# Moving one chunk's attention work between the first MLP blocks, with more blocks on three chunks and a second weight slice in halves

## The chip, the cores and the metric

One core of one Trainium2 chip. The metric is device time in microseconds (us) of one execution. The profile's span, first to last instruction, is 1.7 to 1.8 us shorter than the device time of the same execution.

## The reference

Lightning attention with decay (8 heads, 4 sequences of 768, head size 64), then an MLP with exact GELU over the 3072 tokens:

```python
for b in range(nb):                                # blocks of 64 in the reference, chunks of 128 in the kernel
    intra = (q_b @ k_b.T * Dmask) @ v_b
    inter = (q_b * lam_pow) @ kv_state
    out[b] = intra + inter
    kv_state = lam_block * kv_state + (k_b * rev_pow).T @ v_b
# ...
x = out as [3072, 512]
return gelu(x @ w_in) @ w_out                      # w_in 512x2048, w_out 2048x512
```

## The kernel before

A chunk is 128 tokens of one sequence. Group 0 is the first chunk of each of the four sequences (chunks 0 to 3), group 1 the second (4 to 7), and so on to group 5. Each group's 512 tokens go through 16 MLP blocks (`mm1`, one per 128 columns of w_in, each followed by GELU on ScalarE) and then the second matmul (`mm2`). Attention of the next group is put between blocks by `visits`: a visit at `(g, i)` runs in front of block `i` of group `g`. The program order of each engine is the order of the text. The first four blocks of groups 0 and 1 run on three chunks (384 columns); the fourth chunk's 128 columns follow in one block of their own, the catch-up.

In groups 0 and 1 a chunk takes TensorE transposes of k and q, a copy of kT (ScalarE), a scaling of qT (VectorE), scores, masked scores (VectorE), outputs, and a copy of the outputs into `x_t` (ScalarE). From group 2 on the transposes are made by DMA and the copy by VectorE. The state products (`kv`) multiply the decayed k (`decay_k`) with v and update `kv_state`. The dummy matmuls of `keep_warm` only keep TensorE busy; with fewer of them (experiments 2, 7 and 8) the granted clock was still 1.00 over the first 32 us.

```python
    for item in "q0 k1 q1 k2 q2 v1 v2 k3 q3".split():
        load(int(item[1]), item[0])
# ...
    load_w_in(0, 2)
    load_w_in(2, 4)
    load(3, "v")
    for s in range(4, NK2, 4):
        load_w_in(s, s + 4)
# ...
        split = g < 2
        def mm1(kf, lo=0, n_kf=1):
            hi = T - C if split and kf < NK2 // NS and lo == 0 else T   # first 4 blocks: three chunks
# ...
        if split:
            blocks.insert(NK2 // NS, mm1(0, T - C, NK2 // NS))          # the catch-up with the fourth chunk
# ... the opening, after chunks 0 and 1:
    outputs(live[1])
    keep_warm(2)                 # dummy matmuls
    transposes(live[3])
    outputs(live[2])
    keep_warm(1)
    scores(live[3])
    keep_warm(4)
    for n in range(M):
        decay_k(live[n], nc.vector)
    make_lam_blk()
# ...
    def first_requests():                       # visit (0, 30)
        for n in (2 * M, 2 * M + 1):
            request(n)                          # GpSimd scales q, DMA transposes k and q
        for n in range(M, 2 * M):
            decay_k(live[n], nc.gpsimd)
```

## Time and profile before

| | kernel before |
|---|---|
| device time, first three runs | 214.65 us (214.28 to 214.77) |
| span of the profiled execution | 213.1 us |
| TensorE busy | 96% |
| MLP's first block starts | 18.34 us |
| block 4 starts (20.08, then blocks 2 and 3, 8 x 0.1625, and the catch-up, 16 x 0.056) | 22.28 us |
| block 8 starts (24.88, then state products, 0.44, and block 7, 0.86) | 26.18 us |

The order of instructions on TensorE, with the idle time and its releaser in brackets, tells what waited; the time from issue to landing of a load tells what could have waited. A load is asked for alone by a window around its issue, and its landing is the issue time plus the "to landing" figure. The prediction below shows those lines.

### The profile page before, as it was taken

Reading aid. Unit: us, or ns where it says so; the run is one execution under the profiler, and the core shown is the slowest. Engines: PE = TensorE matmul, PEld = TensorE weight load, DVE = VectorE, ACT = ScalarE, POOL = GpSimd, SP = SyncE. Lnnn points to the kernel's source line nnn. Section 1 sums busy time; section 2 is a strip of 40 time slices with the busy share of each in tenths; the row PEclk is TensorE's granted clock in tenths of the full one; section 3 lists DMA queues with packets and bytes.
Section 4 is the critical chain, followed back from the end, with each engine's and each line's share of the span. In section 5 each row is a group of like instructions: output and inputs, shape, how many; then the busy total and the mean of one; then the engine's idle time right before and its main releaser. Section 6 shows DMA issues by size and latency. Waiting matters only on the chain.

```text
span 213.1 us, 3522 instructions
## 1 busy us (share of the span) xinstructions
PE 204.4 (96%) x1429; PEld 104.8 (49%) x1455; DVE 76.9 (36%) x122; ACT 87.3 (41%) x152; POOL 103.3 (48%) x118
## 2 busy tenths in 40 slices
PE   7969999999999999999999999999999999999993
PEld 2535554465655445445445445445445445444452
DVE  4758320165293747138317137217132312000000
ACT  5564663343656111464321464321465221576121
POOL 7995333892997965939678795830000000000000
PEclk9999999999999999999999999999999999999999
DMA  7999999999999699999989999991330012100112
GB/s 85 141 150 196 206 206 186 154 211 142 178 87 119 72 108 115 205 167 101 136 128 157 172 131 142 130 117 67 108 74 0 3 65 82 49 3 0 49 51 97
DMA packets 100799, 24.48 MB, mean 115 GB/s; under 512 B 92976, under 2 KB 97840, under 8 KB 100784
## 3 DMA queue, kind: packets, MB, share of 16 engines
q0 software_dynamic: 78592, 13.51, 87.1%
q1 hardware_dynamic: 22192, 10.76, 24.8%
q8 instruction: 11, 0.18, 0.4%
q14 instruction: 4, 0.03, 0.1%
HBM read 27.27 MB, written 6.29 MB: 157 GB/s over the span
## 4 chain that ended last, share of the span: by engine, by line
PE 89%; POOL 4%; DMA 3%; issue 1%; DVE 1%; ACT 0%; POOLq 0%
PE h_ps L263 39%; PE o_ps L275 37%; DMA q_t<-in_q_dram 3%; PE o_ps L230 3%; PE sc_ps L197 3%; PE o_ps L224 2%; PE kv_ps L209 2%; POOL k_t L66 2%; PE o_ps L290 2%; POOL q_t L66 1%; PE t_ps L176 1%; POOL v_t L66 1%; DVE qT L182 1%; PE idle_ps L325 0%; ACT o_sb L294 0%
## 5 line engine op out<-in xcount | busy, mean ns | idle before, releaser
L263 PE MATMUL h_ps<-x_t,w_in_t 128*128 128x512 bf16 (+2 forms) x404 | 85.7, 362 | 0.6
L275 PE MATMUL o_ps<-w_out_t,g_t 128*128 128x512 bf16 x356 | 81.7, 379 | 1.0 <-issue 0.6
L265 ACT ACTIVATE g_t<-h_ps 128x512 bf16<-128x512 f32 (+1 forms) x98 | 57.7, 588 | 37.2 <-PE h_ps L263 37.0
L263 PEld LDWEIGHTS <-w_in_t 128*128 128x128 bf16 x416 | 38.5, 98 | 41.7
L275 PEld LDWEIGHTS <-g_t 128*128 128x128 bf16 x368 | 34.7, 98 | 41.1
L201 DVE TENSOR_TENSOR sc_m<-sc_ps,dmask 128x512 bf16<-128x512 f32 x48 | 30.1, 683 | 35.0 <-PE sc_ps L197 35.0
L280 ACT COPY o_sb<-o_ps 128x512 f32<-128x512 f32 x23 | 13.5, 585 | 69.9 <-PE o_ps L275 66.4
L189 POOL TENSOR_TENSOR q_hat<-q_t,lam_p 128x512 bf16<-128x512 bf16 x16 | 16.8, 1052 | 24.1 <-DMA q_t<-in_q_dram 13.6
L66 POOL DMA_DIRECT2D k_t<-in_k_dram x24 | 22.1, 919 | 5.4 <-DMA w_out_t<-in_moe_w_out_dram 1.6
L66 POOL DMA_DIRECT2D q_t<-in_q_dram x24 | 21.6, 901 | 4.4 <-DMA w_out_t<-in_moe_w_out_dram 3.3
L66 POOL DMA_DIRECT2D v_t<-in_v_dram x23 | 20.9, 911 | 3.5 <-DMA w_out_t<-in_moe_w_out_dram 1.7
L216 DVE TENSOR_TENSOR tmp<-kv_ps,state 128x512 f32<-128x512 f32 x16 | 11.0, 686 | 31.2 <-PE kv_ps L209 31.2
L169 POOL TENSOR_TENSOR k_dec<-k_t,lam_m 128x512 bf16<-128x512 bf16 x16 | 17.2, 1104 | 0.0
L236 DVE CAST x_t<-o_ps 128x512 bf16<-128x512 f32 x16 | 10.3, 682 | 10.2 <-PE o_ps L230 10.2
L217 DVE TENSOR_TENSOR state<-tmp,lam_blk 128x512 bf16<-128x512 f32 x16 | 12.6, 790 | 0.6
L325 PE MATMUL idle_ps<-idle 128*128 128x512 bf16 x29 | 10.7, 478 | 1.2 <-DVE idle L105 1.2
L182 DVE TENSOR_TENSOR qT<-t_ps,lam_q 128x512 bf16<-128x512 bf16 x8 | 5.5, 691 | 15.4 <-PE t_ps L176 15.0
L197 PEld LDWEIGHTS <-kT 64*128 64x128 bf16 x192 | 5.7, 94 | 6.5 <-issue 3.8
L197 PE MATMUL sc_ps<-qT,kT 64*128 64x128 bf16 x192 | 8.2, 218 | 0.6 <-DVE qT L182 0.2
L230 PE MATMUL o_ps<-sc_m,v_t 128*64 128x128 bf16 x192 | 8.6, 223 | 0.1
L181 ACT COPY kT<-t_ps 128x512 bf16<-128x512 bf16 x8 | 4.7, 584 | 7.4 <-PE t_ps L176 7.4
L230 PEld LDWEIGHTS <-v_t 128*64 128x64 bf16 x192 | 5.9, 109 | 2.7 <-issue 0.6
(41 smaller groups left out, 73.4 us busy)
## 6 DMA issues: line engine op xcount, KB each, us to landing
out_dram<-o_sb SPq DMA_DIRECT2D x23, 256.0 KB, 2.2
k_t<-in_k_dram POOLq DMA_DIRECT2D x24, 128.0 KB, 5.1
q_t<-in_q_dram POOLq DMA_DIRECT2D x24, 128.0 KB, 6.0
v_t<-in_v_dram POOLq DMA_DIRECT2D x23, 128.0 KB, 6.0
w_out_t<-in_moe_w_out_dram POOLq DMA_DIRECT2D x4, 512.0 KB, 16.6
w_in_t<-in_moe_w_in_dram POOLq DMA_DIRECT2D x3, 512.0 KB, 11.0
w_in_t<-in_moe_w_in_dram POOLq DMA_DIRECT2D x2, 256.0 KB, 7.1
v_f<-in_v_dram SPq DMA_DIRECT2D x1, 256.0 KB, 3.6
```

Of the source, the lines that this page charges most:

```text
L66: nc.gpsimd.dma_start(raw[n, name], chunk_of(name, n))
L169: eng.tensor_mul(c.k_dec, c.k, lam_m[:, :, None].to_broadcast((128, H, D)))
L189: nc.gpsimd.tensor_mul(q_hat, c.q, lam_p[:, :, None].to_broadcast((128, H, D)))
L197: nc.tensor.matmul(sc_ps[hi][:, hp, :], c.kT[p, hp, :], c.qT[p, hp, :], start=True, stop=True)
L201: nc.vector.tensor_mul(c.sc_m[:, :, hi, :], sc_ps[hi], dmask_r[:, :, hi, :])
L216: nc.vector.tensor_add(tmp, kv_ps, states[c.b])
L217: nc.vector.tensor_mul(new, tmp, lam_blk)
L230: nc.tensor.matmul(c.o_ps[hi * D:(hi + 1) * D, hp, :], c.v[:, 2 * hp + hi, :], c.sc_m[:, hp, hi, :], start=(c.so == 0 and hp == 0), stop=T ...
L263: nc.tensor.matmul(h_ps[:, f, :], w, x_t[:, ki, lo:hi], start=(ki == 0 and f == 0), stop=(ki == NK1 - 1), skip_group_check=True)
L265: nc.scalar.activation(g_t[:, kf:kf + n_kf, lo:hi], h_ps, ACT.Gelu)
L275: nc.tensor.matmul(om[io], g_t[:, kf, io * C:(io + 1) * C], w_out_t[:, kf, :], start=(kf == 0), stop=(kf == NK2 - 1))
L280: nc.scalar.copy(o_sb, om[io])
```

## The change

Its intent is to open the MLP earlier. Chunk 3's transposes and scores, which the first blocks don't need, move between the blocks. So that this doesn't put the catch-up with chunk 3 too early, eight blocks of group 0 rather than four run on three chunks, with two catch-ups. The weights of blocks 4 to 7 come in two loads, as the earlier opening wants blocks 4 and 5 sooner. The dummies become one group of nine. The diff in full:

```diff
--- before.py
+++ after.py
@@ -96,8 +96,8 @@
     load_w_in(0, 2)
     load_w_in(2, 4)
     load(3, "v")
-    for s in range(4, NK2, 4):
-        load_w_in(s, s + 4)
+    for lo, hi in [(4, 6), (6, 8), (8, 12), (12, 16)]:
+        load_w_in(lo, hi)
     for s in range(NS):
         load_w_out(s)
 
@@ -248,13 +248,13 @@
     def mlp_blocks(g):
         T = M * C
 
-        split = g < 2
+        split = {0: 8, 1: 4}.get(g, 0)
         x_t = xT[g]
         g_t = g_pool.tile([128, NK2, T], BF16, tag="g", name="g_t")
 
         def mm1(kf, lo=0, n_kf=1):
 
-            hi = T - C if split and kf < NK2 // NS and lo == 0 else T
+            hi = T - C if kf < split and lo == 0 else T
             def run():
                 h_ps = bank([128, n_kf, hi - lo], F32, "m", "h_ps")
                 for f in range(n_kf):
@@ -297,8 +297,8 @@
 
         parts = NK2 // 4
         blocks = [mm1(kf) for kf in range(NK2)]
-        if split:
-            blocks.insert(NK2 // NS, mm1(0, T - C, NK2 // NS))
+        for i, kf in enumerate(range(0, split, 4)):
+            blocks.insert(split - 1 + 2 * i if split > 4 else split, mm1(kf, T - C, 4))
         if g == 0:
 
             blocks += [(mm2(io, part), 4 * 512) for pair in range(0, M, 2) for part in range(parts)
@@ -348,14 +348,8 @@
     keep_warm(2)
     outputs(live[1])
     keep_warm(2)
-    transposes(live[3])
     outputs(live[2])
-    keep_warm(1)
-    scores(live[3])
-    keep_warm(4)
-    for n in range(M):
-        decay_k(live[n], nc.vector)
-    make_lam_blk()
+    keep_warm(9)
 
 
     for n in range(M, 2 * M + 2):
@@ -380,6 +374,11 @@
         for n in ns:
             next_state(live[n])
             take_state(live[n])
+
+    def late_decays():
+        for n in range(M):
+            decay_k(live[n], nc.vector)
+        make_lam_blk()
 
     def first_requests():
         for n in (2 * M, 2 * M + 1):
@@ -392,17 +391,19 @@
 
 
     visits = {
-        (0, 2): [lambda: outputs(live[3])],
-        (0, 8): [lambda: kv(0, 1)],
-        (0, 11): [lambda: kv(2, 3)],
-        (0, 25): [lambda: transposes(live[4])],
-        (0, 26): [lambda: scores(live[4])],
-        (0, 27): [lambda: transposes(live[5]), lambda: outputs(live[4])],
-        (0, 28): [lambda: scores(live[5])],
-        (0, 29): [lambda: transposes(live[6]), lambda: outputs(live[5])],
-        (0, 30): [lambda: scores(live[6]), lambda: first_requests()],
-        (0, 31): [lambda: transposes(live[7]), lambda: outputs(live[6])],
-        (0, 32): [lambda: scores(live[7])],
+        (0, 2): [lambda: transposes(live[3])],
+        (0, 3): [lambda: scores(live[3]), late_decays],
+        (0, 6): [lambda: outputs(live[3])],
+        (0, 10): [lambda: kv(0, 1)],
+        (0, 13): [lambda: kv(2, 3)],
+        (0, 26): [lambda: transposes(live[4])],
+        (0, 27): [lambda: scores(live[4])],
+        (0, 28): [lambda: transposes(live[5]), lambda: outputs(live[4])],
+        (0, 29): [lambda: scores(live[5])],
+        (0, 30): [lambda: transposes(live[6]), lambda: outputs(live[5])],
+        (0, 31): [lambda: scores(live[6]), lambda: first_requests()],
+        (0, 32): [lambda: transposes(live[7]), lambda: outputs(live[6])],
+        (0, 33): [lambda: scores(live[7])],
         (1, 1): [lambda: outputs(live[7])],
         (1, 5): [lambda: kv(4, 5)],
         (1, 7): [lambda: kv(6, 7)],
```

## The prediction

> **What bounds the kernel now.** I read the page first (busy shares, slices, chain), then the chain of waits from 0 to 60 us, then the order of instructions from 13 to 26.6 us, then the time from issue to landing of single loads. Of the page:
>
> ```profile
> PE 204.4 (96%) x1429; PEld 104.8 (49%) x1455; DVE 76.9 (36%) x122; ACT 87.3 (41%) x152; POOL 103.3 (48%) x118
> PE   7969999999999999999999999999999999999993
> PEclk9999999999999999999999999999999999999999
> PE 89%; POOL 4%; DMA 3%; issue 1%; DVE 1%; ACT 0%; POOLq 0%
> ```
>
> TensorE is 96% busy at full clock and makes 89% of the chain that ends last. Only the first three slices (16 us) have room. After 18.3 us TensorE waits for nothing worth naming, so a gain must be made before that and survive until the steady stream of weights and tokens. The chain there (start, duration, what):
>
> ```profile
> 9.63 6.28 DMA q_t<-in_q_dram
> 15.96 0.41 PE t_ps L176 x4
> 16.39 0.70 DVE qT L182
> 17.14 0.40 PE sc_ps L197 x8
> 17.91 0.59 PE idle_ps L325 x2
> 18.51 1.30 PE h_ps L263 x8
> ```
>
> The MLP opens only when chunk 3 is through: its q lands (15.9), is transposed, scaled by VectorE, scored, and four dummy matmuls follow. But the first MLP blocks use chunks 0 to 2 alone. The order of instructions shows it (start, duration, engine, line, operation, count, idle before):
>
> ```profile
> 13.66 0.60 PE L325 MATMUL idle_ps<-idle 128*128 128x512 bf16 x2
> 14.11 0.39 PE L176 MATMUL t_ps<-ident,k_t 128*128 128x128 bf16 x4
> 15.96 0.40 PE L176 MATMUL t_ps<-ident,q_t 128*128 128x128 bf16 x4 [1.47 <-DMA q_t<-in_q_dram]
> 16.29 0.41 PE L230 MATMUL o_ps<-sc_m,v_t 128*64 128x128 bf16 x8
> 16.74 0.58 ACT L234 CAST x_t<-o_ps 128x512 bf16<-128x512 f32 x1 [1.63 <-PE o_ps L230]
> 18.34 1.46 PE L263 MATMUL h_ps<-x_t,w_in_t 128*128 128x384 bf16 x8
> 19.74 0.41 PE L230 MATMUL o_ps<-sc_m,v_t 128*64 128x128 bf16 x8
> 20.23 0.58 ACT L234 CAST x_t<-o_ps 128x512 bf16<-128x512 f32 x1
> 24.88 0.61 PE L209 MATMUL kv_ps<-v_t,k_dec 128*128 128x128 bf16 x8
> ```
>
> Chunk 2's outputs (16.29) stand in program order behind the wait for chunk 3's q, though VectorE finished chunk 2's masked scores at 12.61 + 1.88 = 14.49. What else could hold the MLP is its weights. The first w_in slice, asked for by itself, shows:
>
> ```profile
> L90 POOL DMA_DIRECT2D w_in_t<-in_moe_w_in_dram x1: 834/834/834, 10.5 to 10.5; - x1
> DMA to landing us min/median/max: 6.8/6.8/6.8
> ```
>
> Issued at 10.49, landed at 17.29. That is only 1.05 us before the MLP's present start. The same view gives the others: slice blocks 2-3 at about 18.5, v of chunk 3 at 19.7, blocks 4-7 at 12.84 + 9.2 = 22.0, blocks 8-11 at 24.6, 12-15 at 27.0. So 256 KB of w_in take about 1.2 us of a queue that is backlogged throughout (206 GB/s).
>
> **What the Trainium skill says.** "TensorE: Matmul & The Clock Gate", section "Wait — 56ns, not 53.3ns?": warm back-to-back matmuls start every N/2.4 + 2.5 ns. The trace agrees: eight of 384 columns take 1.30 us (162 each), twelve of 512 take 2.59 us (216), and eight of 128 take 0.45 us (56). The same page, "HAM oscillation — how this bites in real kernels": the clock falls after idle gaps of some 3.4 us. Here the gap of 1.47 us left the granted clock at 1.00, and the change makes none so long. "ScalarE: Activation LUTs", "What ACT_TABLE_LOAD costs": an activation costs a fixed part plus 0.833 ns a column, and neighbours overlap by some 93 ns. Here 384 columns take 0.49 us, 512 take 0.60, and successive starts overlap by 0.10. "DMA: Bandwidth & Descriptors", "Anatomy of one DMA — SWDGE (gpsimd) path", gives about 2 us fixed per transfer. In this backlog landings come 1.2 us apart, so that fixed part overlaps, and halving a load should not cost it again; no run shows that yet.
>
> **The change part by part.** Let S be the start of the MLP; the place to compare is the start of block 8 with both versions having done the state products of chunks 0 and 1. In the kernel before that is 24.88 + 0.44 (state products) + 0.86 (block 7) = 26.19.
>
> Removed in front of S: chunk 3's transposes (8 x 56 ns = 0.45), the 1.47 us wait, the wait for qT, scores (0.33), and five dummies, against nine dummies in one group. Chunk 2's outputs can now start at 14.49 + 0.05 = 14.55 and take 0.34; nine dummies take 9 x 0.216 = 1.94, to 16.83. ScalarE's copy of chunk 2 ends near 15.6. The first weights land at 17.29, so S is about 17.33, set by the weights and not by the dummies. Gain at S: 18.34 - 17.33 = 1.01.
>
> Added after S: transposes 0.45 and scores 0.33 = 0.78, merely moved. The second catch-up: four blocks become 16 x 162 ns + 16 x 56 ns instead of 16 x 216 ns, that is 2.60 + 0.90 - 3.45 = 0.05. Work after S up to block 8: eight blocks 8 x 0.65 = 5.20, transposes 0.45, scores 0.33, outputs 0.34, two catch-ups 1.80, state products 0.45: 8.57, against 7.75 before (18.34 to 26.19 is 7.85, with 0.10 of waiting for v).
>
> New waits after S, by program order:
> Transposes run S+1.30 to S+1.75, block 2 to S+2.40. The q transposes of chunk 3 started at 15.96 before and their scores at 17.14, 1.18 later; now they start at S+1.52, so scores can start at S+2.70. Wait 0.30. (ScalarE copies kT after the activation of block 1, ending near S+2.5, earlier than that.)
> Scores to S+3.03, block 3 to S+3.68 = 21.0. Blocks 4-5 now need a half slice: 19.7 + 1.2 = 20.9. Wait about 0. With the whole slice at 22.0 it would have been 1.0, which is what the halving is for. Blocks 6-7 land near 22.1, wanted at 22.6.
> Outputs of chunk 3 at S+4.98; their x comes 0.45 later plus a copy of 0.58, but ScalarE is in the activation of block 5 from S+5.18 for 0.49. With the overlap of 0.10 the copy runs S+5.57 to S+6.15. TensorE has finished block 6 at S+5.97, so the first catch-up starts near S+6.22. Wait 0.25.
> Sum: 8.57 + 0.30 + 0.25 = 9.12; block 8 at 17.33 + 9.12 = 26.45, that is 0.26 later than 26.19. The decays of k move behind chunk 3's scores on VectorE; from S+4.4 they take 2.49 + 0.58 to S+7.5 = 24.8, and the state products want them near S+8.2. Off the path. Block 8's weights (24.6) are there. From here both kernels have the same work, so the end moves by the same amount.
>
> **The rivals.**
> A, the waits are smaller than I count: if TensorE loses nothing after S, block 8 starts at 25.90 and the kernel gains 0.29, to 214.35. For it: VectorE is idle before qT and the wait of 0.30 is a difference of small numbers. Against it: the 1.18 us from transposes to scores is measured on this very chunk.
> B, the whole 1.8 us between the early outputs and the old start is won (dummies end at 16.83, S there, and little is given back): 213 or so. Against it: the weights at 17.29. The queue ahead of them is unchanged, so they cannot come sooner.
> C, the extra load delays others. GpSimd runs at most eight loads open: the second w_out waits for q, the third for the first w_in, always eight back. One more load shifts w_out's first issue by a microsecond, yet all of these then sit in a backlog and land when the bytes ahead are through. Group 1's q of chunk 4 lands at 22.32 + 16.8 = 39.1 and is used at 40.45, 1.3 us of slack. If half loads move bytes more slowly by a fifth, blocks 4-5 wait some 0.3 and the time is 215.2.
> D, ScalarE becomes the bound among the first blocks: six activations of 0.49 with two copies of 0.58 need 4.1 of the first 6 us. Against it: a third is free.
>
> **Range and chances.** The sum says +0.26; A pulls down by up to 0.55, C up by 0.3, and the three runs before span 0.49. I predict 214.85 us, with 214.2 to 215.5 to hold it eight times in ten. Two per cent is 4.3 us; even a complete removal of everything idle before 18.34 is below that. Faster by over 2%: 0.01; within 2%: 0.98; slower: 0.01.
>
> **What would show it.** In the changed trace: outputs of chunk 2 near 14.55; a short idle stretch before the first MLP block ended by the w_in load, block at 17.3; 0.3 us idle before chunk 3's scores, released by VectorE's qT; about none before block 4; 0.25 idle before the first catch-up, released by ScalarE's copy of x; the state products of chunks 0 and 1 near 26.0 and block 8 near 26.45; the rest of the kernel equal, only shifted. I am wrong if S is well under 17.3 (the weights came sooner), if the second half slice makes TensorE wait, or if loads of chunks 4 and 5 run late near 40 us.

## The result, and the profile after

| | before | after |
|---|---|---|
| device time, median of four runs | 214.47 us (214.25 to 214.77) | 214.88 us (214.53 to 215.05) |
| span of the profiled execution | 213.1 us | 213.3 us |
| first w_in slice landed | 17.3 us | 16.3 us |
| MLP's first block starts | 18.34 us | 16.88 us |
| block 4 starts | 22.28 us | 20.91 us |
| block 8 starts | 26.18 us | 26.32 us |

The ratio of after to before is 1.0016, 95% interval 0.9997 to 1.0036: the same.

The page of the changed kernel: busy times first, then the chain's shares. TensorE still sets the time, but the chain now has 4% of DMA for w_in.

```profile
PE 205.5 (96%) x1450; PEld 105.9 (50%) x1475; DVE 77.7 (36%) x122; ACT 87.4 (41%) x153; POOL 104.0 (49%) x119
...
PE 88%; POOL 5%; DMA 4%; issue 1%; ACT 0%; POOLq 0%
```

The order of instructions in the opening (start, duration, engine, line, operation, count, idle before):

```profile
14.27 0.73 PE L230 MATMUL o_ps<-sc_m,v_t 128*64 128x128 bf16 x8
...
14.93 1.90 PE L325 MATMUL idle_ps<-idle 128*128 128x512 bf16 x8
...
16.88 1.46 PE L263 MATMUL h_ps<-x_t,w_in_t 128*128 128x384 bf16 x8
...
18.63 0.81 PE L263 MATMUL h_ps<-x_t,w_in_t 128*128 128x384 bf16 x4
...
18.83 0.69 DVE L182 TENSOR_TENSOR qT<-t_ps,lam_q 128x512 bf16<-128x512 bf16 x1 [4.27 <-PE t_ps L176]
...
19.57 0.40 PE L197 MATMUL sc_ps<-qT,kT 64*128 64x128 bf16 x8
...
20.91 1.47 PE L263 MATMUL h_ps<-x_t,w_in_t 128*128 128x384 bf16 x8 [0.18 <-DMA w_in_t<-in_moe_w_in_dram]
...
22.31 0.41 PE L230 MATMUL o_ps<-sc_m,v_t 128*64 128x128 bf16 x8
...
22.66 3.38 PE L263 MATMUL h_ps<-x_t,w_in_t 128*128 128x384 bf16 x40
...
25.87 0.61 PE L209 MATMUL kv_ps<-v_t,k_dec 128*128 128x128 bf16 x8
```

The MLP opens 1.46 us sooner, at the end of the dummies. (The view counts eight of the nine; some records of matmuls are missing in a trace.) From 16.88 to 26.32 are 9.44 us, of which 8.57 are work (the prediction's sum). The scores wait: block 2 is through at 18.63 + 0.65 = 19.28 and they start at 19.57, 0.29 lost. Block 3 is through at 19.91 + 0.65 = 20.56 and block 4 starts at 20.91, 0.35 lost. (The bracket says 0.18 because the ends of matmuls are modelled with their latency; starts and known spacing are the safer count.) Blocks 4 and 5 take 1.30, so the outputs at 22.31 come 0.10 late. The forty matmuls from 22.66 to 25.87 are 3.10 us of work in 3.21. That gives 0.29 + 0.35 + 0.10 + 0.11 = 0.85, and 8.57 + 0.85 = 9.42.

The chain of waits (start, duration, what) says the same in three lines. It runs back from block 4 to the issue of the load at 12.86. Nothing that TensorE did before 20.9 is on it:

```profile
12.86 8.01 DMA w_in_t<-in_moe_w_in_dram
20.86 0.05 issue
20.91 1.47 PE h_ps L263 x8
```

After block 8 both executions are alike. The last group of matmuls starts at 206.12 before and at 206.25 after, 0.13 later, as block 8 did (0.14).

### The profile page after: what moved, and what is told of

Read it like the earlier page. It is cut to its first block, busy times and chain, and to the rows that moved or that the text cites. A ratio compares the mean times of both kernels' runs of the same rounds, so it can differ in the third digit from the quotient of the medians.

```text
span 213.3 us, 3565 instructions
## 1 busy us (share of the span) xinstructions
PE 205.5 (96%) x1450; PEld 105.9 (50%) x1475; DVE 77.7 (36%) x122; ACT 87.4 (41%) x153; POOL 104.0 (49%) x119
## 4 chain that ended last, share of the span: by engine, by line
PE 88%; POOL 5%; DMA 4%; issue 1%; ACT 0%; POOLq 0%
PE h_ps L263 38%; PE o_ps L275 37%; DMA w_in_t<-in_moe_w_in_dram 4%; PE o_ps L230 3%; PE sc_ps L197 3%; PE kv_ps L209 2%; PE o_ps L224 2%; POOL k_t L66 2%; PE o_ps L290 2%; POOL q_t L66 2%; POOL v_t L66 1%; PE t_ps L176 1%; POOL w_in_t L90 1%; ACT o_sb L294 0%; POOL row L78 0%
## 5 line engine op out<-in xcount | busy, mean ns | idle before, releaser
L263 PEld LDWEIGHTS <-w_in_t 128*128 128x128 bf16 x432 | 39.2, 98 | 41.5 <-DMA w_in_t<-in_moe_w_in_dram 0.6
L66 POOL DMA_DIRECT2D k_t<-in_k_dram x24 | 22.1, 919 | 5.5 <-DMA w_in_t<-in_moe_w_in_dram 2.9
L66 POOL DMA_DIRECT2D q_t<-in_q_dram x24 | 21.6, 900 | 3.9 <-DMA w_out_t<-in_moe_w_out_dram 3.4
L169 POOL TENSOR_TENSOR k_dec<-k_t,lam_m 128x512 bf16<-128x512 bf16 x16 | 17.3, 1107 | 0.0
L217 DVE TENSOR_TENSOR state<-tmp,lam_blk 128x512 bf16<-128x512 f32 x16 | 13.5, 841 | 0.6
## 6 DMA issues: line engine op xcount, KB each, us to landing
w_out_t<-in_moe_w_out_dram POOLq DMA_DIRECT2D x4, 512.0 KB, 16.4
```

The source lines that it names most:

```text
L66: nc.gpsimd.dma_start(raw[n, name], chunk_of(name, n))
L169: eng.tensor_mul(c.k_dec, c.k, lam_m[:, :, None].to_broadcast((128, H, D)))
L217: nc.vector.tensor_mul(new, tmp, lam_blk)
L263: nc.tensor.matmul(h_ps[:, f, :], w, x_t[:, ki, lo:hi], start=(ki == 0 and f == 0), stop=(ki == NK1 - 1), skip_group_check=True)
```

## The experiments

Twelve experiments ran, five rounds each, in four calls; three of them repeat a kernel (before, after, combined). All gave correct results. Times are set against the kernel before in the same rounds; its medians were 214.76, 214.68, 214.19 and 214.86 us, with single runs from 213.91 to 216.22. Times therefore resolve about 0.3%. What is smaller is read from the traces.

This table is from one profiled execution of each. "Landed" is the load that brings block 4's weights. Block 8 starts with the state products of chunks 0 and 1 done; where these stand ahead of block 7, its start is worked out as in the table of before. "Rest" is the span minus block 8's start.

| kernel | first slice landed | MLP starts | block 4's weights landed | block 4 starts | block 8 starts | span | rest |
|---|---|---|---|---|---|---|---|
| before | 17.3 | 18.34 | 22.0 | 22.28 | 26.18 | 213.1 | 186.9 |
| after | 16.3 | 16.88 | 20.9 | 20.91 | 26.32 | 213.3 | 187.0 |
| scores later | 16.1 | 16.92 | 20.7 | 20.72 | 26.13 | 213.1 | 187.0 |
| six dummies | 16.4 | 16.49 | 20.7 | 20.68 | 26.09 | 213.2 | 187.1 |
| whole slice | 17.1 | 17.20 | 21.9 | 21.92 | 27.33 | 214.3 | 187.0 |
| v later | 15.6 | 17.01 | 19.5 | 20.68 | 26.09 | 213.0 | 186.9 |
| before, again | 16.3 | 17.32 | 22.1 | 22.16 | 26.06 | 213.0 | 186.9 |
| after, again | 17.2 | 17.24 | 21.7 | 21.79 | 27.20 | 214.1 | 186.9 |
| combined | 16.3 | 16.34 | 19.0 | 19.82 | 25.23 | 212.9 | 187.7 |
| before, no dummies | 17.0 | 17.17 | 21.6 | 21.74 | 25.64 | 212.6 | 187.0 |
| scores of 8, 9 later | 17.0 | 17.00 | 19.6 | 20.49 | 25.90 | 212.8 | 186.9 |
| decays on VectorE | 16.8 | 16.84 | 19.4 | 20.32 | 25.73 | 212.9 | 187.2 |
| combined, again | 16.3 | 16.36 | 19.1 | 19.84 | 25.25 | 212.8 | 187.6 |
| decays first | 16.6 | 16.67 | 20.2 | 20.28 | 25.87 | 214.5 | 188.6 |

Theory 1 was that the arrival of block 4's weights fixes block 4, so that a head start runs into it. Theory 2 was that every wait and every microsecond of head start counts by itself.

### 1. Scores one block later

```diff
-        (0, 3): [lambda: scores(live[3]), late_decays],
+        (0, 4): [lambda: scores(live[3]), late_decays],
```

> The changed kernel with chunk 3's scores one block later (after block 3 instead of after block 2). Theory 1 (the arrival of w_in blocks 4-5 near 20.9 us fixes block 4): the 0.29 us in which TensorE waits for kT/qT before the scores goes, the wait before block 4 grows by the same, block 4 still starts when its weights land, 20.9 +- 0.2, and the time is that of the changed kernel within 0.1 us (about 214.9). Theory 2 (each wait is a loss of its own): about 0.3 us faster than the changed kernel, about 214.6.

Measured: 214.68 us, ratio to the kernel before 0.9997 (0.9972 to 1.0023). The wait for qT before the scores is gone (0.09 us is left between block 3 and the scores). TensorE then waits for the weights, the time from the end of the scores, 20.06 + 0.33 = 20.39, to 20.72, when they land at 20.7. Block 8 is 0.19 us earlier than after, and all of it is that in this execution the load landed 0.2 sooner. Theory 1 holds in the trace; the times alone couldn't have told a gain of 0.3 us.

### 2. Six dummies

```diff
-    keep_warm(9)
+    keep_warm(6)
```

> The changed kernel with six instead of nine dummy matmuls before the MLP. In the changed kernel's trace the MLP opened at 16.88 because the dummies ended there; its first weights had landed at 16.3. Theory 1 (arrival of blocks 4-5 fixes block 4): the MLP opens up to 0.5 us earlier, the wait before block 4 grows by as much, time unchanged within 0.1 us (214.9). Theory 2 (the start of the MLP carries through): 0.4 to 0.6 us faster, about 214.4.

Measured: 214.84 us, 1.0007 (0.9978 to 1.0035). In order of instructions:

```profile
16.49 1.47 PE L263 MATMUL h_ps<-x_t,w_in_t 128*128 128x384 bf16 x8
...
19.53 0.82 PE L263 MATMUL h_ps<-x_t,w_in_t 128*128 128x384 bf16 x4
20.68 1.48 PE L263 MATMUL h_ps<-x_t,w_in_t 128*128 128x384 bf16 x8 [0.33 <-DMA w_in_t<-in_moe_w_in_dram]
```

The MLP opens 0.39 us before the changed kernel's and waits 20.68 - 20.18 = 0.50 at block 4 instead of 0.35. The rest of the 0.39 is the landing, 0.2 earlier. The head start is swallowed.

### 3. The second slice whole

```diff
-    for lo, hi in [(4, 6), (6, 8), (8, 12), (12, 16)]:
+    for lo, hi in [(4, 8), (8, 12), (12, 16)]:
```

> The changed kernel without the halving of the second w_in slice: blocks 4-7 in one load. Theory 1: block 4 waits for the whole slice, landing 22.0 to 22.2 instead of 20.9, so block 4 starts 1.1 to 1.3 us later; of this nothing is made up later, time about 216.0 (0.5% slower than the changed kernel). Theory 2 (weights are not what binds, only the moved work and split blocks cost): same time as the changed kernel within 0.2 us.

Measured: 215.86 us, 1.0051 (1.0025 to 1.0078), slower than the kernel before clear of noise. In order of instructions:

```profile
21.92 1.47 PE L263 MATMUL h_ps<-x_t,w_in_t 128*128 128x384 bf16 x8 [0.86 <-DMA w_in_t<-in_moe_w_in_dram]
```

Block 4 starts 1.01 us later than after, block 8 1.01 later, and the span is 1.0 longer. In the same rounds experiments 1 and 2, which keep the halving, took 214.68 and 214.84, so the whole slice costs 1.0 to 1.2 us. One pair of landings would not show this, as experiment 6 will tell. But over the four profiles with this load whole (before twice, experiments 3 and 8) it landed at 21.6 to 22.1, 21.9 in the mean, and over the four with the half in the same place (after twice, experiments 1 and 2) at 20.7 to 21.7, 21.0 in the mean. This is the cleanest of the set: moving one landing moves the end by about as much, and without the halving the other parts of the change lose time.

### 4. v of chunk 3 after blocks 4 and 5

```diff
-    load(3, "v")
-    for lo, hi in [(4, 6), (6, 8), (8, 12), (12, 16)]:
+    load_w_in(4, 6)
+    load(3, "v")
+    for lo, hi in [(6, 8), (8, 12), (12, 16)]:
```

> The changed kernel with v of chunk 3 loaded after w_in blocks 4-5 instead of before. v is wanted only at 22.3 us. Theory 1: blocks 4-5 land about 1.1 us sooner (about 19.8), the wait of 0.35 us before block 4 goes, block 8 starts near 26.0 instead of 26.3, time about 0.35 us less than the changed kernel (214.5). Theory 2 (weights not binding): unchanged. A third outcome: v or blocks 6-7 (landing 22.2) become the next wait and take back part of the 0.35.

Measured: 214.79 us, 1.0009 (0.9982 to 1.0037). The weights landed at 19.5 and the wait for them is gone: no DMA wait of TensorE from 10 to 60 us. Yet block 4 started at 20.68, as in experiments 1 and 2. Here the MLP opened at 17.01 behind nine dummies, and 2.60 of blocks, 0.78 of transposes and scores and the 0.29 for qT make 20.68:

```profile
20.03 2.12 PE L264 MATMUL h_ps<-x_t,w_in_t 128*128 128x384 bf16 x12
```

Those twelve matmuls are blocks 3 to 5, without a gap. So two paths reached block 4 near 20.7 at once: the landing of its weights, and TensorE's own sequence, which holds the dummies and the wait for qT. Experiments 1 and 2 shorten the second path only, this one the first only, and each time the other is left.

### 5 and 6. Both kernels again

> The kernel before, unchanged, as a control: how far two sets of runs of the same program differ, and how much the landing of the same loads moves between executions. Time within 0.3 us of the kernel before. If the landings of the first w_in slice (17.3 in the first trace) and of blocks 4-7 (22.0) move by some tenths of a us while the rest of the trace does not, then the 1.0 us by which the changed kernel's first slice came sooner is chance of the execution and not the change; if they land at 17.3 and 22.0 again, within 0.1, it is the change.

> The changed kernel, unchanged, on the same chip as the others of this call. Time 214.9 +- 0.3, within 0.2% of the kernel before. Landing of blocks 4-5 between 20.5 and 21.0, block 4 at once after it, block 8 at 26.1 to 26.4.

Measured: before 214.79 us, 0.9995 (0.9966 to 1.0024); after 214.79 us, 1.0009 (0.9979 to 1.0040). Here are the first slice and the slice of blocks 4-7 in the second execution of the kernel before; each figure is from an issue at 10.5 and at 12.8:

```profile
L90 POOL DMA_DIRECT2D w_in_t<-in_moe_w_in_dram x1: 834/834/834, 10.5 to 10.5; - x1
DMA to landing us min/median/max: 5.8/5.8/5.8
...
L90 POOL DMA_DIRECT2D w_in_t<-in_moe_w_in_dram x1: 862/862/862, 12.8 to 12.8; - x1
DMA to landing us min/median/max: 9.3/9.3/9.3
```

So the first slice came at 16.3, a full microsecond before the 17.3 of the first execution of the same program, while the next one came at 22.1 against 22.0. The early landing in the changed kernel's trace was chance: this kernel, with the same loads ahead, has it too. TensorE in this execution opened the MLP 1.02 us earlier (17.32) and started block 4 only 0.12 earlier (22.16). That is Theory 1 again, in a kernel without the change:

```profile
22.16 2.77 PE L263 MATMUL h_ps<-x_t,w_in_t 128*128 128x512 bf16 x11 [0.72 <-DMA w_in_t<-in_moe_w_in_dram]
```

The changed kernel had the reverse luck in its second profile. The first slice landed at 17.2 and blocks 4-5 at 21.7, outside the 20.5 to 21.0 that was expected. TensorE waited for both (0.77 and 0.69 by the brackets), block 8 came at 27.20 against an expected 26.1 to 26.4, and the span was 214.1:

```profile
17.24 1.47 PE L263 MATMUL h_ps<-x_t,w_in_t 128*128 128x384 bf16 x8 [0.77 <-DMA w_in_t<-in_moe_w_in_dram]
...
21.79 1.47 PE L263 MATMUL h_ps<-x_t,w_in_t 128*128 128x384 bf16 x8 [0.69 <-DMA w_in_t<-in_moe_w_in_dram]
```

That execution took 215.90 us where its neighbours took 214.39 to 215.70. So the 0.8 us between the spans of the two profiled executions of this kernel come from the landing of blocks 4-5, 0.8 later; what scatters the runs without a profile isn't shown.

### 7. All three together

The edits of 1, 2 and 4 in one:

```diff
-    keep_warm(9)
+    keep_warm(6)
# ...
-        (0, 3): [lambda: scores(live[3]), late_decays],
+        (0, 4): [lambda: scores(live[3]), late_decays],
# ...
+    load_w_in(4, 6)
     load(3, "v")
-    for lo, hi in [(4, 6), (6, 8), (8, 12), (12, 16)]:
+    for lo, hi in [(6, 8), (8, 12), (12, 16)]:
```

> The changed kernel with all three: six dummies, scores one block later, v after blocks 4-5. Theory 1 (each of these only frees time when the weights of blocks 4-5 come sooner): MLP opens at 16.4 +- 0.3, no wait for scores, block 4 at S+3.4 = 19.8, no wait for blocks 6-7 (landing near 21.2, wanted at 21.6), block 8 near 25.5, that is 0.6 us before the changed kernel with v later alone and 0.7 before the kernel before: 214.0 +- 0.3. Theory 2 (something later fixes the time, so that no head start reaches the end): 214.7 like all the others, with a new wait later, for the loads of chunks 4 and 5 near 40 us or for blocks 8 to 15.

Measured: 214.44 us, 0.9983 (0.9958 to 1.0009). The MLP opened at 16.34, right behind its weights, block 4 started at 19.82 and block 8 at 25.23, 0.95 before the kernel before. That is as Theory 1 expects, and it holds to 61 us. But only 0.2 of it reached the end. In order of instructions, TensorE, then VectorE, then GpSimd:

```profile
61.44 0.45 PE L198 MATMUL sc_ps<-qT,kT 64*128 64x128 bf16 x9
62.35 0.38 PE L198 MATMUL sc_ps<-qT,kT 64*128 64x128 bf16 x7 [0.45 <-DVE tmp L217]
```

```profile
57.27 1.58 DVE L218 TENSOR_TENSOR state<-tmp,lam_blk 128x512 bf16<-128x512 f32 x1
58.76 0.68 DVE L217 TENSOR_TENSOR tmp<-kv_ps,state 128x512 f32<-128x512 f32 x1
```

```profile
53.25 1.04 POOL L190 TENSOR_TENSOR q_hat<-q_t,lam_p 128x512 bf16<-128x512 bf16 x1 [1.40 <-DMA q_t<-in_q_dram]
54.25 4.04 POOL L170 TENSOR_TENSOR k_dec<-k_t,lam_m 128x512 bf16<-128x512 bf16 x4
```

The scores of chunks 8 and 9 stop in the middle until VectorE has read a PSUM tile that they reuse. VectorE is late because one product took 1.58 us, where the same operation took 0.69 in the kernel before:

```profile
58.23 0.69 DVE L217 TENSOR_TENSOR state<-tmp,lam_blk 128x512 bf16<-128x512 f32 x1
```

In the combined kernel it ended at 58.85, 0.56 after GpSimd's four decays of k (54.25 + 4.04 = 58.29). And those start when q of chunk 9 lands (near 53.2) and has been scaled. The Trainium skill, page "SBUF — State Buffer", section "SBUF: two separate sides", says that VectorE, in an operation with two SBUF inputs, and GpSimd, in one that reads SBUF, hold a common port pair exclusively, and that the one who comes second blocks. The product is of that kind (`tmp` and `lam_blk`), the fourth decay started at about 57.28 (54.25 + 3/4 of 4.04), just as the product did, and the product ended 0.56 after it. That fits; but in experiment 9 a product that began 0.16 us before the last decay ended took only 0.70. No run here isolates it.

So there is a second gate. Neither theory was whole: the head start counts once the weights let it, and then it meets a load again, at 53 us (experiments 9 to 12 test this).

### 8. The kernel before without its last four dummies

```diff
     scores(live[3])
-    keep_warm(4)
```

> The kernel before without the four dummy matmuls (0.87 us) between chunk 3's scores and the MLP. Theory 1 (weights fix block 4): the MLP opens at 17.5, then waits for v of chunk 3 before its outputs and for blocks 4-7 (landing about 22.0; block 4 started at 22.29), so at most 0.3 us is gained, 214.4 against 214.65. Theory 2 (the start of the MLP carries through): 0.87 us gained, 213.8.

Measured: 214.77 us, 0.9994 (0.9966 to 1.0022). Theory 2's 0.87 us would be a ratio of 0.9959, just outside the interval; the point estimate is a gain of 0.13 us. In the trace the MLP opened at 17.17 straight after the scores. TensorE waited 0.55 by the bracket before chunk 3's outputs, which started at 19.19, and reached block 4 at 21.74 (19.19 + 0.34 + 1.30 + 0.90), when its weights had been there since 21.6. So here v of chunk 3 and not the weights held block 4. It is 0.54 us earlier than in the first execution of before, more than the 0.3 expected, because v landed at 19.2 and not 19.7 and the slice 0.4 earlier. One thing to learn from its brackets: TensorE's list of waits calls the 0.55 a wait for VectorE's k_dec, while the list for the weight loads has 0.9 us of DMA for v. The matmul needs no k_dec, and v landed at 12.0 + 7.2 = 19.2. It is v.

### 9. Scores of chunks 8 and 9 later, on the combined kernel

```diff
-        add(g, a0, lambda n=n: pair_a(n))
+        add(g, a0 + (2 if g == 1 else 0), lambda n=n: pair_a(n))
```

> The combined kernel of the run before, with the scores of chunks 8 and 9 two MLP blocks later in group 1; their loads stay where they were. In the combined kernel TensorE was 0.96 us ahead of the kernel before from 25 to 61 us and lost about 0.7 of it in one place, at 61.9 to 62.35, waiting in those scores for a PSUM bank that VectorE's state update gives back; VectorE stood at the same times as in the kernel before. Theory 3 (that one wait is where the head start goes): no wait near 62, the lead of 0.9 us kept to the end, 213.8 +- 0.3, some 0.6 us under the combined kernel. Rival (there is always a next wait, for loads or VectorE, further on): the wait comes back at another place before 110 us and the time stays at 214.4.

Measured: 214.25 us, 0.9995 (0.9968 to 1.0022); the combined kernel in the same rounds 214.21. The wait near 62 us did not occur, but in this profile the first slice landed at 17.0, so block 8 had a lead of only 0.28, and that was kept (rest 186.9). The profile can't say whether a lead of 0.95 would pass. The times show no gain over the combined kernel, where 0.6 us was expected; but 0.6 us is 0.28%, no more than the interval's reach to either side. Theory 3, that this one wait is where the head start goes, isn't supported.

### 10. Two decays on VectorE, on the combined kernel

```diff
-        for n in range(M, 2 * M):
+        for n in range(M, M + 2):
             decay_k(live[n], nc.gpsimd)
# ...
-        (1, 1): [lambda: outputs(live[7])],
+        (1, 1): [lambda: outputs(live[7]), lambda: [decay_k(live[n], nc.vector) for n in (6, 7)]],
```

> The combined kernel with the scores of chunks 8 and 9 where they were, but two of the four decays of k (chunks 6 and 7) on VectorE, which is idle there, instead of GpSimd. In the combined kernel VectorE's first state product at 57.27 took 1.58 instead of 0.69 us and ended 0.55 after GpSimd's decays ended (58.29). If the two cannot run at once (Theory 4), GpSimd's decays now end near 56.3, the state product takes 0.69 to 0.8, the bank comes back 0.6 to 0.9 us sooner, and TensorE's wait near 62 goes: 213.8 +- 0.3. If the stretched state product has another cause, it stays at 1.58 and the time at 214.4.

Measured: 214.64 us, 1.0009 (0.9990 to 1.0027), no better than the combined kernel. GpSimd's two decays ended at 54.43 + 2.49 = 56.92, 1.4 us sooner but 0.6 later than expected, and the first product took 0.69. But later products were stretched in its place: 1.23 us at 59.09, while GpSimd was issuing loads, and 1.41 at 62.40, while it decayed chunks 8 and 9. The two decays on VectorE themselves took 2.13 us, and a scaling on GpSimd beside them 1.58 instead of 1.04. The lead at block 8 was 0.45, of which 0.2 reached the end. This fits operations of the two engines blocking one another. But the product stretched while GpSimd only issued loads (and one of 1.30 at 57.91 in experiment 12, in the same situation) shows that the decays aren't the whole of it. The move doesn't help.

### 11. The combined kernel again

> The combined kernel once more, on the same chip and in the same rounds as the other two, so that they can be set against it: 214.4 +- 0.3, with the wait of 0.4 to 0.7 us in the scores near 62 us.

Measured: 214.21 us, 0.9992 (0.9974 to 1.0010). Block 8 came at 25.25, a lead of 0.93; at the end 0.3 was left. The expected wait near 62 us wasn't there. The lead went earlier, at the two state products of 56.14 and 58.62, which took 0.92 and 0.89 us instead of 0.61, and the list of the weight loads' waits names the reason:

```profile
PEld L210 <- POOL k_dec L170: 0.6, 2, 0.3
```

GpSimd's decays ran until 54.57 + 4.49 = 59.06 in this execution. So the same late decays take the lead in two ways, here directly, in experiment 7 by way of VectorE.

### 12. Decays ahead of the scaling, on the combined kernel

```diff
     def first_requests():
+        for n in range(M, 2 * M):
+            decay_k(live[n], nc.gpsimd)
         for n in (2 * M, 2 * M + 1):
             request(n)
-        for n in range(M, 2 * M):
-            decay_k(live[n], nc.gpsimd)
```

> The combined kernel with GpSimd's four decays of chunks 4 to 7 ahead of its two scalings of q (chunks 8 and 9) instead of behind them. GpSimd sat idle for 3.2 us there waiting for q of chunk 8, and its decays ended at 58.3 to 59.1 after q of chunk 9 landed near 53.2, whatever TensorE's lead. Theory 5 (that landing, through the decays, fixes the state products of chunks 4 to 7 and so gives the lead back): decays end near 52 to 53, no wait in the state products at 56 to 59 nor in the scores near 62, TensorE's lead over the kernel before at block 8 (0.3 to 0.95 us, by the landing of its weights) is kept to the end, median 213.8 +- 0.3, about 0.4 us under the combined kernel. Rival (the lead is lost elsewhere, or the late scaling of q makes chunks 8 and 9 the next wait): 214.2 or more, with a wait near 62 or 74.

Measured: 216.54 us, 1.0088 (1.0060 to 1.0116), slower clear of noise. The first half of the expectation came true: the decays ran from 48.76 to 52.81 and the state products waited for nothing. The rival came true too. The scalings of q for chunks 8 and 9 now started at 52.77, the DMA transposes of qT were issued at 53.83 and 56.43 instead of 52.16 and 54.76, and the scores of chunk 9 waited:

```profile
63.93 0.40 PE L198 MATMUL sc_ps<-qT,kT 64*128 64x128 bf16 x8 [1.47 <-DMA qT<-q_hat]
```

That second transpose took 7.37 us from issue to landing, where it took 2.8 in the kernel before; from 54.75 to 60.05 GpSimd issued six loads of 128 KB, which in the kernel before began at 58.24. That these loads slowed the transpose isn't isolated. The lead at block 8 was only 0.31 here: the weights of blocks 6 and 7 landed at 22.3, and TensorE waited 0.3 us for them. So the run shows what the old order is good for. Between 48 and 62 us GpSimd's work has two deadlines, the decays before the state products at 56 to 59 and the scaling in time for its transposes and the scores at 61.4 to 62, and in the two orders tried one of the two is late once TensorE is ahead. With the scores of 8 and 9 also moved (experiment 9) there may be an order that meets both; it wasn't run.

## Why the prediction was right or wrong

The time was right (214.85 predicted, 214.88 measured), though it was predicted from the first three runs of the kernel before (214.65), and the ratio's interval, 0.9997 to 1.0036, doesn't settle that there is a loss. Right too was the reading that a head start of more than a microsecond would be given back before block 8. Block 8 was predicted at 26.45 and came at 26.32. That both agree so closely is luck. In the second profile (experiment 6) the start was as predicted, 17.24 behind weights that landed at 17.2, and block 8 came at 27.20, 0.75 later than predicted, since the half slice landed at 21.7. Taken step by step, with the first profile:

- **The start of the MLP.** Predicted 17.33, set by the weights; measured 16.88, set by the dummies, the weights having landed at 16.3. The end of the dummies was predicted at 16.83, so that sum was right. The step that failed is the claim in rival B that they cannot come sooner. Experiment 5 shows that the landing varies by a microsecond between executions of one program. Over all fourteen profiles it lies between 15.6 and 17.3, and the page that the prediction was made from has the latest of them. It isn't the chip alone: on the chip of experiments 1 to 4 the landings are 15.6 to 17.1.
- **The wait for qT before the scores.** Predicted 0.30, measured 0.29.
- **The weights of blocks 4 and 5.** Landing predicted at 20.9, measured 20.9, but by another way: v landed at 18.6 rather than 19.7, and the half slice came 2.3 us behind it rather than 1.2. So the rate of 256 KB in 1.2 us didn't hold for this load. The wait was sized at about 0 and was 0.35. It is this term that took back most of the 0.45 won at the start; experiments 2 and 3 show that the landing, not the start, fixes block 4.
- **Chunk 3's outputs and the first catch-up.** Predicted 0 and 0.25; measured 0.10 and 0.11 for the stretch that holds the catch-up. The 0.10 ahead of these outputs stood in the kernel before too, where the prediction put it down to v. That was a misreading: it is there in every profile but that of experiment 8, also where v had landed 3.7 us earlier (18.6, outputs at 22.31). What it is isn't shown. ScalarE's copy of x started at 22.81, 0.50 after the outputs, and the sum of the two waits is near enough.
- **Moved and added work.** Predicted 8.57 in all, and it balances to 0.02 us with the four waits read off the trace. So the extra catch-up can't cost much more than the 0.05 that was said; no run isolates it.
- **The halving.** Predicted worth about 1.0; experiment 3 measured 1.0 to 1.2 in time, and the landings differ by 0.9 in the mean.
- **The rest of the kernel only shifted.** Right for this change: the rest is 186.9 to 187.0 us in both executions of both kernels. It would have been wrong for a larger gain: at a lead of 0.93 to 0.95 (experiments 7 and 11) the rest grew to 187.6 and 187.7. Rival C, a delay of later loads by the extra load, didn't show: TensorE of the changed kernel has no DMA wait between block 4 and 60 us. Of the others, A (nothing lost after S) fails on the 0.85 us that were lost, and D (ScalarE as the bound) on the 0.11 that is all TensorE lost in the stretch that holds the wait for ScalarE's copy.

None of the versions tried beats the kernel before clear of noise. The combined one comes nearest, with 0.9983 and 0.9992, both intervals reaching over 1. What remains open is which order of GpSimd's work from 48 to 62 us would let a lead of 0.95 us through, what makes the first loads land up to 1.7 us apart, and what stretches VectorE's products while GpSimd only issues loads.

## What to carry to other kernels

A head start in front of a stage that eats a stream of loads is worth little until the load that the stage reaches next comes sooner too: list the landing of every load beside the time at which each block wants it, and move the landing first. When several things hold the same instruction, taking one away shows no gain; find them all, and then look for the next gate before counting the sum as won. Before trusting a landing to some tenths of a microsecond, profile the same program twice.

## What the Trainium skill lacked or had wrong

- "TensorE: Matmul & The Clock Gate", section "Back-to-back issue gap", gives about 131 ns a matmul of 512 columns and 81 ns of 128 as the sustained rate of a real stream, and says that its own formula of N/2.4 + 2.5 over-counts at 512. Here the streams, with a weight load for each matmul, hold 216 ns at 512 columns (12 in 2.59 us) and 56 at 128 (8 in 0.45 us): the formula is right, the sustained figures are not, for this kernel.
- "DMA: Bandwidth & Descriptors", section "Anatomy of one DMA — SWDGE (gpsimd) path", gives a transfer as a fixed 2 us plus bytes, with no word on spread. The first w_in load, with the same queue ahead of it, took 5.8 and 6.8 us to land in two executions of the kernel before, and 5.1 to 6.8 over all profiles.
- The same section's fixed part can't be added per load in a backlog: in the four profiles with blocks 4-5 and 6-7 loaded one right after the other the two halves landed 1.2 to 1.4 us apart (20.9 and 22.2 in the changed kernel), not 2 us and more.
- "SBUF — State Buffer", section "SBUF: two separate sides", has the port that VectorE and GpSimd share. It agrees with the 1.58 us product of experiment 7. The products of 1.23 us in experiment 10 and 1.30 in experiment 12, while GpSimd was only issuing loads, aren't told there as a case in which VectorE is the one that waits; no run here separates the cause.
